# Linear attention and mixer in one kernel: batch 0's residual taken from a turned copy instead of from TensorE, with a new order of the engines' work

## The chip, the cores and the metric

The kernel runs on one core of a Trainium2 chip. The metric is device time in microseconds (us): one launch, as the slowest (here the only) core takes it.

## The reference

Inputs are `r`, `k`, `v` of shape 4 x 8 x 768 x 48 (batch, heads, steps, head size), the decay `w` and the bonus `u` (8 x 48), and four mixer weights. For each batch and head a state of 48 x 48 runs over the steps:

```
y[t]  = r[t] @ (state + (u*k[t]) outer v[t])
state = w * state + k[t] outer v[t]
```

The heads' outputs, side by side, are `x` (4 x 768 x 384). The mixer follows:

```
h   = relu(x^T @ w_tok1) @ w_tok2      # over the 768 steps, hidden 256
u   = x + h^T
out = u + relu(u @ w_ch1) @ w_ch2      # over the 384 channels, hidden 1536
```

The output is float32; TensorE works in bf16.

## The kernel before, in words

A batch's 768 steps are six chunks of 128. A chunk (or, for batch 0, a pair of chunks at once) goes through: products of `k` and `r` with decay tables (`kr`, on POOL or VectorE), a turn of them so that channels lie on partitions (by TensorE into `tr_ps`/`trk` for batches 0 and 1, by a DMA transpose `turn_rk` into `rk` for batches 2 and 3), scores on TensorE (`at_ps`) and their mask on VectorE (`AT`), the state's update (`kv_ps`), and the output `y_ps`, which ends as `x_b`.

The mixer of a batch follows: `hid` (h_ps, six chunks by w_tok1), a ReLU to `h1r`, then per half of the batch (sg = 0, 1, three chunks each) the sum `u`. Where `(b, sg)` is in `DIRECT`, TensorE makes `u` turned: `turn_x` and `back` into `hx_ps`, copied to `uT`. Elsewhere `back` makes `hT_ps`, VectorE adds `x_b` into `u_sb`, and the DMA transpose `turn_u` on SP's queue turns it into `uT`. From `uT` come twelve `up` groups a half (three matmuls of 128 x 384 each, `z_ps`, then a ReLU to `zr`), and three output tiles a half, each of three `down` groups of four matmuls (`h_ps`; the group that begins at j0 uses weight block w4, w5 or w6 for j0 = 0, 4, 8). The output tile still lacks the residual `u`. It comes in one of two ways:

```
by_res = [direct[sg] and (b, sg) not in BACK for sg in range(2)]
# by_res: in down(), after the last group, three matmuls of uT with the identity into the same bank;
#         sum_o() is then a copy, on ScalarE or VectorE as ENGINES says
# else:   sum_o() is a VectorE add of h_ps and u_sb; where the half is DIRECT, u_sb is uT turned back:
def turn_back(sg):
    def f():
        M["u", sg] = sb("u_sb", [128, 3, dm], bf16)
        sp.dma_start_transpose(M["u", sg].rearrange("p c (m d) -> p (c m) d", m=3),
                               M["uT", sg].rearrange("p c m t -> p (c m t)"))
    return f
```

The order of everything is written out. The code adds 880 tasks (a task is a few instructions of one engine), numbered as they are added; `ORDER` (line 22) lists the numbers, and the tasks are emitted in that order and kept in it on every engine, on POOL's queue and on SP's, which issues all loads, stores and transposes. `BUFS` gives the buffer of each allocation, `ENGINES` the engine of each task that may run on two. `WAITS` (line 130) makes some DMAs wait for others: the load of batch 1's first v tile waits for weight block w2, for instance. `FILL` (line 139) adds matmuls on a constant tile `warm` ahead of the tasks it names. The seven weight transfers w0 to w6 (w0, w1 tokens; w2, w3 up; w4 to w6 down) are issued by POOL, in its order with its products.

Numbers that come up later, in the old numbering: 116 and 117 are w5 and w6; 318 is the product of k of batch 1, chunk 1, 63 its load, 62 the load of v of batch 1, chunk 0; 599 is the `back` of batch 2, chunk 4, 603 the `turn_u` of batch 2, second half, 604 and 628 the first `up` of its two halves; 781 is the last `back` of batch 3, 783 the `turn_u` of its second half, 784 and 808 the first `up`s.

Of the kernel before, what the change touches and what calls it, by code (L numbers as in the profile page):

```python
# [62 lines left out]
    0, 1, 2, 3, 4, 5, 0, 1, 2, 3, 5, 4, 0, 1, 3, 2, 5, 4, 0, 1, 3, 5, 4, 2,  # L63
    ],
# [8 lines left out]
    ],  # L73
    'kp': [
    0, 1, 2, 3, 4, 5, 1, 3, 4, 0, 2, 5, 3, 2, 1, 4, 5, 2, 1, 3, 0, 5, 4, 1, 3, 2, 0,
    ],
    'p': [
    0, 1, 2, 3, 4, 5, 0, 2, 0, 3, 1, 4, 2, 0, 5, 3, 1, 4, 2, 0, 5, 3, 4, 1,
    ],
    'a': [  # L80
    0, 1, 2, 3, 4, 5, 6, 7, 8, 9, 10, 2, 0, 1, 4, 3, 6, 7, 5, 10, 2, 8, 9, 3, 1, 0, 4, 6, 7, 2, 5, 8, 10, 9, 3, 2, 7,
    8, 1, 0, 4, 6, 5, 10, 3, 2, 9, 7, 1, 8, 0, 4, 10, 6, 5, 9, 2, 7, 3, 0,
    ],
    'e': [
    0, 1, 2, 3, 4, 5, 6, 7, 8, 9, 10, 11, 0, 1, 2, 3, 4, 5, 10, 9, 0, 2, 6, 8, 7, 3, 4, 10, 2, 6, 8, 7, 9, 10, 2, 3,
    4, 6, 7, 9, 6, 8, 4, 11, 7, 5, 9, 8, 6, 4, 7, 0, 6, 7, 9, 8, 7, 11, 0, 9, 6, 8, 7, 5, 10, 3, 2, 11, 0, 1, 9, 6, 8,
    7,
# [8 lines left out]
    0, 1, 2, 3, 4, 5, 6, 7, 8, 9, 10, 11, 0, 2, 1, 3, 4, 5, 6, 7, 8, 9, 10, 11, 1, 3, 5, 6, 0, 8, 9, 2, 4, 7, 10, 11,  # L96
    ],
    'g': [
    0, 1, 2, 3, 4, 5, 0, 1, 2, 4, 3, 5, 0, 1, 2, 3, 0, 4, 1, 2, 5,
# [5 lines left out]
    0, 1, 2, 3, 4, 5, 6, 1, 0, 2, 3, 4, 5, 6, 1, 2, 0, 4, 3, 5, 6, 2, 1, 4,  # L105
    ],
    'u': [
    0, 1, 2, 3, 4, 5, 6, 7, 1, 0, 2, 5, 4, 3,
# [6 lines left out]
    ],  # L115
}
ENGINES = [
# [18 lines left out]
WIDE_AT = [  # L136
    0, 1, 2, 3, 4, 5, 6, 7, 8, 9, 10, 11, 12,
]
FILL = {132: 3, 140: 3, 206: 1, 879: 1}
POOL_ONLY = [2, 3]  # L140
PAIRED = [(0, 0), (0, 1), (0, 2)]
GB = [2, 2, 3, 3]
# [13 lines left out]
PART = 4  # L156
STORE = ['SP', 'SP', 'SP', 'SP']
WIDE_K = [2, 3]
BACK = [(1, 0)]
MASK_LATER = []  # L160
END = 256
CAST = []
# [1093 lines left out]
```

## Time and profile before

| | |
|---|---|
| runs | 159.94, 159.95, 160.15 us; median 159.95 |
| span of the profiled execution | 158.2 us (its own time is one of those above; about 1.75 us lie around the span) |
| instructions | 4001 |
| busy in the span | TensorE 151.8 us, VectorE 107.0, POOL 90.1, ScalarE 77.7 |
| DMA | 27.39 MB, mean 173 GB/s |
| granted TensorE clock | 0.998 of full speed |

PE is TensorE's matmuls, PEld its weight loads, DVE is VectorE, ACT ScalarE, POOL GpSimd, SP SyncE; a q behind an engine is its queue or sequencer. All instructions stand on line 239, the helper that records the order, so groups and waits are told apart by their tiles (out<-in). A row of the timeline or of the chain begins with its start and its length; in square brackets stands how long the engine was idle before it and what ended that. Rows of groups end with busy time, mean length in ns, idle time before and its cause. A matmul's length holds its way through the array; how far apart they start is seen from row to row.

### The profile page before, as it was taken

To read this page: it belongs to the slowest core of one execution; us is meant where nothing else is said; L and a number is where in the kernel's file an instruction comes from. 1 tells how busy PE (TensorE), PEld (TensorE's weight loads), DVE (VectorE), ACT (ScalarE), POOL (GpSimd) and SP (SyncE) were. 2 spreads that over 40 slices of the span, in tenths; PEclk is the share of its full clock that TensorE was granted. 3 is DMA by queue.
4 is the path that set the end of the run, shared out by engine and by line. 5 is a ranking of instruction groups with operands and counts; after the bars stand their busy time and mean duration, and the time that the engine had idled before them with its cause. 6 is when DMAs were issued, how large, how long until landed. Compare 5 with 4: busy or idle time off the path is not lost.

```text
span 158.2 us, 4001 instructions
## 1 busy us (share of the span) xinstructions
PE 151.8 (96%) x1574; PEld 101.3 (64%) x1574; DVE 107.0 (68%) x218; ACT 77.7 (49%) x187; POOL 90.1 (57%) x120
## 2 busy tenths in 40 slices
PE   6988999999999999999999999999999999999991
PEld 1356767776767676666677665576666566666660
DVE  2689992468967994467989637898987465432071
ACT  3677797737990581478476440235643102463000
POOL 7859969444183799999928999398920000000000
PEclk9999999999999999999999999999999999999999
DMA  4999999999989999999999989999992075300044
GB/s 125 265 261 264 205 204 210 229 204 210 227 176 187 203 230 195 187 210 136 220 194 173 227 158 129 190 193 215 145 274 101 29 176 146 126 0 4 0 151 147
DMA packets 88148, 27.39 MB, mean 173 GB/s; under 512 B 82753, under 2 KB 87234, under 8 KB 88130
## 3 DMA queue, kind: packets, MB, share of 16 engines
q1 hardware_dynamic: 85776, 23.86, 76.1%
q0 software_dynamic: 2160, 3.15, 11.7%
q8 instruction: 12, 0.20, 0.5%
q10 hardware_dynamic: 194, 0.14, 0.3%
q14 instruction: 6, 0.05, 0.1%
HBM read 20.65 MB, written 4.72 MB: 160 GB/s over the span
## 4 chain that ended last, share of the span: by engine, by line
PE 87%; DVE 4%; DMA 3%; POOL 2%; ACT 1%; issue 1%; POOLq 0%; ACTq 0%
PE h_ps L239 35%; PE z_ps L239 29%; PE y_ps L239 6%; PE at_ps L239 4%; PE kv_ps L239 3%; PE hT_ps L239 3%; PE hx_ps L239 3%; DVE kr L239 3%; DMA uT<-u_sb 3%; PE tr_ps L239 2%; PE ad_ps L239 1%; PE trk L239 1%; POOL mask L239 1%; ACT rka L239 1%; POOL bm L239 1%
## 5 line engine op out<-in xcount | busy, mean ns | idle before, releaser
L239 PE MATMUL h_ps<-wch,zr 128*128 128x384 bf16 (+2 forms) x300 | 53.4, 319 | 0.0
L239 PE MATMUL z_ps<-uT,wch 128*128 128x384 bf16 x288 | 52.4, 327 | 0.3 <-DMA uT<-u_sb 0.3
L239 ACT ACTIVATE zr<-z_ps 128x384 bf16<-128x384 f32 x63 | 28.7, 492 | 36.1 <-PE z_ps L239 35.9
L239 PEld LDWEIGHTS <-wch 128*128 128x128 bf16 x288 | 31.1, 114 | 13.4 <-DMA uT<-u_sb 0.7
L239 PEld LDWEIGHTS <-zr 128*128 128x128 bf16 x300 | 27.6, 98 | 15.7
L239 DVE TENSOR_TENSOR AT<-at_ps,mask 128x512 bf16<-128x512 f32 x48 | 30.6, 682 | 2.2 <-PE at_ps L239 2.2
L239 DVE TENSOR_SCALAR zr<-z_ps 128x384 bf16<-128x384 f32 x33 | 17.7, 554 | 13.5 <-PE z_ps L239 13.5
L239 POOL TENSOR_TENSOR yd<-vb,adg 128x384 f32<-128x384 bf16 x13 | 10.6, 829 | 10.8 <-ACT vb L239 5.9
L239 DVE TENSOR_TENSOR osb<-u_sb,h_ps 128x384 f32<-128x384 bf16 (+2 forms) x19 | 10.0, 531 | 9.6 <-PE h_ps L239 9.0
L239 PEld LDWEIGHTS <-kr 128*128 128x128 bf16 (+1 forms) x196 | 11.6, 97 | 3.9 <-DVE kr L239 0.7
L239 POOL TENSOR_TENSOR kr<-rt,wp 128x384 bf16<-128x384 f32 x12 | 12.0, 1005 | 3.1 <-DMA rt<-in_r_dram 3.1
L239 POOL TENSOR_TENSOR ku<-kw,u_bc 128x384 f32<-128x384 f32 x12 | 11.9, 1003 | 2.4 <-DMA u_bc<-in_u_dram 2.4
L239 DVE TENSOR_TENSOR u_sb<-x_b,hT_ps 128x384 bf16<-128x384 bf16 x15 | 7.9, 550 | 6.5 <-PE hT_ps L239 6.4
L239 POOL TENSOR_TENSOR rku<-ku,rt 128x384 f32<-128x384 f32 x12 | 12.0, 1002 | 0.2
L239 POOL TENSOR_TENSOR kr<-kw,wnat 128x384 bf16<-128x384 f32 x12 | 12.0, 1004 | 0.0
L239 ACT CAST vb<-vt 128x384 bf16<-128x384 f32 x18 | 9.0, 513 | 2.5 <-DMA vt<-in_v_dram 2.5
L239 PEld LDWEIGHTS <-wtok 128*128 128x128 bf16 x78 | 7.3, 98 | 4.1
L239 DVE TENSOR_TENSOR x_b<-y_ps,yd 128x384 bf16<-128x384 f32 x18 | 9.4, 551 | 0.6 <-PE y_ps L239 0.5
L239 ACT ACTIVATE yd<-vb,adg 128x48 f32<-128x48 bf16 x40 | 9.5, 322 | 0.1
L239 ACT COPY rkb<-tr_ps 128x1024 bf16<-128x1024 bf16 x6 | 6.1, 1013 | 6.7 <-PE tr_ps L239 6.7
L239 PE MATMUL h_ps<-x_b,wtok 128*128 128x384 bf16 x48 | 8.8, 326 | 0.0
L239 PE MATMUL y_ps<-vb,AT 128*128 128x48 bf16 (+1 forms) x240 | 8.4, 182 | 0.0
(99 smaller groups left out, 190.8 us busy)
## 6 DMA issues: line engine op xcount, KB each, us to landing
out_dram<-osb SPq DMA_DIRECT2D x23, 192.0 KB, 2.6
vt<-in_v_dram SPq DMA_DIRECT2D x18, 192.0 KB, 3.5
win<-in_r_dram SPq DMA_DIRECT2D x6, 384.0 KB, 6.2
kw<-in_k_dram SPq DMA_DIRECT2D x12, 192.0 KB, 4.6
rt<-in_r_dram SPq DMA_DIRECT2D x12, 192.0 KB, 4.0
wch<-in_moe_w_ch_dram POOLq DMA_DIRECT2D x4, 384.0 KB, 6.4
win<-in_k_dram SPq DMA_DIRECT2D x3, 384.0 KB, 5.7
win<-in_v_dram SPq DMA_DIRECT2D x3, 384.0 KB, 7.1
```

The lines of the kernel that those rows point to most:

```text
L239: return lambda *args, **kw: tc.keep_in_program_order(f(*args, **kw))
```

## The change

`BACK` gets both halves of batch 0. So the 18 residual matmuls go, two transposes `turn_back` join SP's queue (the new tasks 219 and 229, which moves all later numbers by 1 and then by 2), and the six evacuations of batch 0 are VectorE adds that also wait for these transposes; four of them were ScalarE copies. `FILL` keeps one entry. The whole `ORDER` is another, with the buffers that go with it, and twelve tasks change engines: the four evacuations (ScalarE to VectorE), `bm` (POOL to VectorE), four products of batch 1 (VectorE to POOL), a copy of batch 1 and two ReLUs of batch 2 (VectorE to ScalarE). Cut to what is spoken of:

```
 ORDER = [
...
-    308, 65, 227, 228, 309, 252, 234, 253, 314, 256, 235, 68, 320, 258, 116, 232, 259, 115, 240, 64, 229, 233, 260,
...
-    73, 315, 264, 316, 239, 275, 317, 262, 265, 251, 341, 343, 266, 117, 342, 326, 267, 329, 327, 50, 270, 67, 351,
...
-    686, 498, 100, 602, 599, 713, 494, 600, 719, 698, 603, 495, 604, 700, 689, 499, 605, 705, 106, 721, 626, 108, 699,
-    610, 694, 290, 716, 618, 706, 703, 622, 619, 724, 628, 623, 608, 629, 714, 616, 725, 500, 614, 609, 646, 617, 745,
...
+    209, 309, 213, 315, 216, 226, 211, 32, 221, 341, 217, 222, 223, 218, 214, 212, 224, 342, 215, 227, 225, 62, 310,
+    228, 73, 230, 311, 63, 254, 236, 255, 316, 37, 234, 50, 237, 65, 272, 48, 235, 262, 231, 320, 343, 273, 263,
...
+    355, 245, 246, 49, 335, 333, 232, 117, 69, 332, 325, 250, 116, 336, 233, 276, 356, 326, 334, 347, 321, 74, 274,
...
+    463, 100, 689, 102, 687, 690, 590, 490, 591, 695, 494, 693, 698, 592, 713, 703, 593, 594, 704, 596, 595, 742,
+    599, 597, 603, 491, 598, 715, 495, 492, 600, 721, 500, 103, 688, 601, 604, 496, 691, 602, 700, 497, 605, 702,
+    501, 696, 630, 106, 708, 606, 716, 701, 626, 108, 607, 631, 628, 718, 292, 624, 502, 104, 717, 625, 726, 612,
...
-FILL = {132: 3, 140: 3, 206: 1, 879: 1}
+FILL = {879: 1}
...
-BACK = [(1, 0)]
+BACK = [(0,0),(0,1),(1,0)]
```

More of the change, by code (lines that the diff above doesn't have):

```diff
@@ L62 @@
     'w': [
-    0, 1, 2, 3, 4, 5, 0, 1, 2, 3, 5, 4, 0, 1, 3, 2, 5, 4, 0, 1, 3, 5, 4, 2,
+    0, 1, 2, 3, 4, 5, 1, 0, 2, 3, 5, 4, 1, 0, 2, 3, 5, 4, 0, 1, 5, 2, 4, 3,
     ],
     'm': [
[7 rows of a table removed]
[7 rows of a table added]
     ],
     'kp': [
-    0, 1, 2, 3, 4, 5, 1, 3, 4, 0, 2, 5, 3, 2, 1, 4, 5, 2, 1, 3, 0, 5, 4, 1, 3, 2, 0,
+    0, 1, 2, 3, 4, 5, 1, 3, 4, 0, 2, 5, 3, 4, 1, 0, 1, 2, 4, 5, 3, 0, 1, 2, 4, 5, 3,
     ],
     'p': [
-    0, 1, 2, 3, 4, 5, 0, 2, 0, 3, 1, 4, 2, 0, 5, 3, 1, 4, 2, 0, 5, 3, 4, 1,
+    0, 1, 2, 3, 4, 5, 1, 3, 2, 1, 0, 2, 4, 3, 5, 1, 0, 2, 4, 3, 1, 5, 2, 0,
     ],
     'a': [
-    0, 1, 2, 3, 4, 5, 6, 7, 8, 9, 10, 2, 0, 1, 4, 3, 6, 7, 5, 10, 2, 8, 9, 3, 1, 0, 4, 6, 7, 2, 5, 8, 10, 9, 3, 2, 7,
-    8, 1, 0, 4, 6, 5, 10, 3, 2, 9, 7, 1, 8, 0, 4, 10, 6, 5, 9, 2, 7, 3, 0,
+    0, 1, 2, 3, 4, 5, 6, 7, 8, 9, 10, 0, 1, 2, 3, 4, 5, 6, 7, 0, 8, 9, 10, 2, 1, 3, 5, 6, 4, 8, 10, 0, 7, 0, 9, 2,
+    4, 8, 1, 3, 5, 6, 10, 2, 7, 0, 9, 1, 4, 3, 8, 5, 6, 2, 10, 0, 9, 1, 7, 3,
     ],
     'e': [
-    0, 1, 2, 3, 4, 5, 6, 7, 8, 9, 10, 11, 0, 1, 2, 3, 4, 5, 10, 9, 0, 2, 6, 8, 7, 3, 4, 10, 2, 6, 8, 7, 9, 10, 2, 3,
-    4, 6, 7, 9, 6, 8, 4, 11, 7, 5, 9, 8, 6, 4, 7, 0, 6, 7, 9, 8, 7, 11, 0, 9, 6, 8, 7, 5, 10, 3, 2, 11, 0, 1, 9, 6, 8,
-    7,
+    0, 1, 2, 3, 4, 5, 6, 7, 8, 9, 10, 11, 0, 1, 2, 3, 4, 5, 9, 8, 10, 0, 11, 6, 5, 1, 0, 5, 3, 0, 9, 11, 6, 1, 3, 0,
+    9, 5, 6, 6, 11, 0, 8, 6, 5, 0, 11, 8, 6, 8, 10, 8, 0, 1, 10, 0, 8, 1, 10, 0, 8, 11, 9, 4, 3, 1, 7, 10, 0, 11, 9,
+    6, 4, 8,
     ],
@@ L95 @@
     'l': [
-    0, 1, 2, 3, 4, 5, 6, 7, 8, 9, 10, 11, 0, 2, 1, 3, 4, 5, 6, 7, 8, 9, 10, 11, 1, 3, 5, 6, 0, 8, 9, 2, 4, 7, 10, 11,
+    0, 1, 2, 3, 4, 5, 6, 7, 8, 9, 10, 11, 0, 3, 2, 1, 5, 6, 4, 7, 8, 9, 10, 11, 3, 0, 2, 1, 6, 5, 4, 7, 8, 9, 10, 11,
     ],
     'g': [
-    0, 1, 2, 3, 4, 5, 0, 1, 2, 4, 3, 5, 0, 1, 2, 3, 0, 4, 1, 2, 5,
+    0, 1, 2, 3, 4, 5, 0, 1, 2, 3, 4, 1, 0, 5, 2, 4, 3, 0, 1, 5, 2,
     ],
@@ L104 @@
     'v': [
-    0, 1, 2, 3, 4, 5, 6, 1, 0, 2, 3, 4, 5, 6, 1, 2, 0, 4, 3, 5, 6, 2, 1, 4,
+    0, 1, 2, 3, 4, 5, 6, 0, 1, 2, 3, 4, 5, 6, 0, 2, 1, 4, 3, 5, 6, 0, 2, 4,
     ],
     'u': [
-    0, 1, 2, 3, 4, 5, 6, 7, 1, 0, 2, 5, 4, 3,
+    0, 1, 2, 3, 4, 5, 6, 7, 0, 1, 3, 2, 4, 7, 6, 5,
     ],
```

97 rows, old and new, of tables (BUFS, ENGINES, ORDER) are left out of this document.

## The prediction

> **What bounds the kernel now.** First the page: the span, the busy shares and the chain that ended last. Then the stretches, to see where TensorE has room.
>
> ```profile
> span 158.2 us, 4001 instructions
> PE 151.8 (96%) x1574; PEld 101.3 (64%) x1574; DVE 107.0 (68%) x218; ACT 77.7 (49%) x187; POOL 90.1 (57%) x120
> PE 87%; DVE 4%; DMA 3%; POOL 2%; ACT 1%; issue 1%; POOLq 0%; ACTq 0%
> 0.00:22.50 22.50, 19.94 (x321) 11.80 (x322) 17.79 (x40) 15.40 (x28) 18.18 (x42) 1.00 1.13 222
> 22.50:45.08 22.58, 22.58 (x252) 16.15 (x252) 15.76 (x33) 17.05 (x41) 11.73 (x14) 1.00 1.09 210
> 45.08:102.47 57.39, 57.09 (x597) 38.59 (x593) 42.12 (x85) 28.16 (x78) 47.42 (x52) 1.00 1.08 189
> 102.47:154.70 52.23, 52.21 (x413) 34.72 (x413) 30.93 (x61) 17.08 (x43) 12.74 (x14) 1.00 0.52 123
> ```
>
> In a row of stretches the first number after the bounds is its length, the next TensorE's busy time; the three last are granted clock, DMA share and GB/s. From 22.5 us to the last matmul TensorE stands still for 0.3 us in 132. So any TensorE work taken out there comes off the time, and any wait put in there is added to it. The DMA share is above 1 up to 102 us: what is issued later than before also lands later. The three runs shown are 159.94 to 160.15 us, median 159.95; the span is 158.2, so 1.75 us lie around it, which I leave as they are. I sum against 159.95.
>
> **What is taken out.** Eighteen 128-column matmuls add the residual of batch 0 (three for each of six output tiles). Seven fill matmuls go too.
>
> ```profile
> 65.24 0.82 PE h_ps L239 x7
> 72.59 0.65 PE h_ps L239 x4
> 10.86 0.81 PE L239 MATMUL at_ps<-warm 128*128 128x512 bf16 x3
> 13.55 0.65 PE L239 MATMUL kv_ps<-warm 128*128 128x384 bf16 x3
> 24.95 0.33 PE L239 MATMUL h_ps<-warm 128*128 128x384 bf16 x1
> 25.12 0.81 PE L239 MATMUL h_ps<-x_b,wtok 128*128 128x384 bf16 x4
> ```
>
> In the chain four down matmuls take 0.65 us, and four with three residual ones 0.82: 0.17 for three, six times, **-1.0 us**. The single fill costs 25.12 - 24.95 = **-0.17**. The other six fills are 0.81 and 0.65 us of TensorE's time, but in a start where it also waits (19.94 of 22.5 us busy); the reordered start (POOL's index patterns ahead of its mask, the decay tables in another order) still needs the same loads and VectorE products. I take **-0.5** for the start, a third of the fills' 1.46 (neither end is nearer by a row), between 0 and -1.5. Sum of the gains: -1.67.
>
> **What is only moved.** Four residual evacuations go from ScalarE copies to VectorE adds (4 x 0.55 = 2.2 us), while four products, a copy and two ReLUs leave VectorE: it is lighter. POOL gets the four products at 1.00 us and loses the mask block `bm`. No TensorE wait hangs on these by itself; cover is POOL's own idle time (4.64 us in the row below). If that cover were gone, the weight DMAs queued on POOL would come later, and that is counted below. The two new turning transfers cost SP an issue each (1.63); the rest of the b=1 and b=2 loads queue behind them, and the six adds wait for them while their h_ps banks stay taken. The cover is whatever slack those loads and banks have, and TensorE's list shows none missing between 45 and 98 us. I take 0 and keep 0 to +1.6, one issue, for the range; less than nothing is excluded, since nothing is loaded sooner by it.
>
> ```profile
> L239 DVE TENSOR_TENSOR osb<-u_sb,h_ps 128x384 f32<-128x384 bf16 x17 | 9.3, 551 | 9.1 <-PE h_ps L239 8.6
> L239 POOL TENSOR_TENSOR kr<-kt,wnat 128x384 bf16<-128x384 f32 x4 | 4.0, 1003 | 0.3 <-POOL kr L239 0.2
> 37.90 0.82 POOL L239 TENSOR_TENSOR yd<-vb,adg 128x384 f32<-128x384 bf16 x1 [4.64 <-ACT adg L239]
> 73.93 1.63 SPq L239 DMA_TRANSPOSE u_sb<-uT  x1
> ```
>
> **The orders: three new waits.** TensorE runs its list in order, so I read the new list (task numbers rise by 1 from 219 and by 2 from 228) for places where less TensorE work stands between a result and its return through another engine and a DMA.
>
> First, batch 2, second half. Before, after its last `back` product come a down group, a score block, `up` of the *first* half, a down group, four more `up`s and a y block, and only then the first `up` of the second half. The new list has ... 496 (down), 700 (scores), 501 (down), 630: task 630 is that `up`, and nothing else is ahead of it.
>
> ```profile
> 97.06 0.49 PE L239 MATMUL hT_ps<-h1r,wtok 128*128 128x384 bf16 x2
> 97.38 0.81 PE L239 MATMUL h_ps<-wch,zr 128*128 128x384 bf16 x4
> 98.13 0.62 PE L239 MATMUL at_ps<-rk 64*128 64x128 bf16 x16
> 98.68 0.68 PE L239 MATMUL z_ps<-uT,wch 128*128 128x384 bf16 x3
> 102.47 3.12 PE L239 MATMUL z_ps<-uT,wch 128*128 128x384 bf16 x18 [0.30 <-DMA uT<-u_sb]
> 94.56 1.37 SPq L239 DMA_TRANSPOSE uT<-u_sb  x1
> 98.17 4.26 DMA uT<-u_sb
> uT<-u_sb SPq DMA_TRANSPOSE x1, 3.9
> ```
>
> From the `back` (97.06) to the `up` (102.47) 5.41 us pass, and even then TensorE waits 0.30: the loop back, add, transfer, up is already the limit here. Of the work ahead there stay 98.68 - 97.06 = 1.62 and one down group of 0.65 (as in the chain): 2.27 us. The transfer took 4.26 us; the last row is the landing of the one issued at 94.56, 3.9. One load fewer is queued ahead of it now, so I take 3.9. The add and the issue come 98.17 - 97.06 = 1.11 after the `back`: 1.11 + 3.9 - 2.27 = **+2.8** (2.0 with 3.2, the quickest landing of such a transfer below, to 3.1). ScalarE and VectorE stand idle behind it; late next is their ReLU, which the following `up`s of both halves cover.
>
> Second, batch 3. The new list goes 663, 674 and 664 in old numbers (down groups), then one `up` of each half less than before: 784, 796, and already 808, the first `up` of the second half.
>
> ```profile
> 127.52 0.49 PE L239 MATMUL hT_ps<-h1r,wtok 128*128 128x384 bf16 x2
> 129.13 1.32 SPq L239 DMA_TRANSPOSE uT<-u_sb  x1
> uT<-u_sb SPq DMA_TRANSPOSE x1, 3.3
> uT<-u_sb SPq DMA_TRANSPOSE x1, 3.2
> 112.17 0.49 PE z_ps L239 x3
> ```
>
> Needed: 129.13 + 3.3 - 127.52 = 4.9 us. There: 0.33 for the `back`, three down groups of 0.65 and two `up`s of 0.49, 3.26. **+1.5** (1.0 if the add is 0.5 us quicker, to 1.7).
>
> Third, the down weights of batch 0. In the new POOL order the second block (`w5`) comes last, after `w6`, behind six products, of which the first (b=1, chunk 1) needs a load that SP now issues after the blocked one.
>
> ```profile
> SPq L239 <- DMA wch<-in_moe_w_ch_dram: 8.3, 1, 8.3
> 13.49 5.51 SPq L239 DMA_DIRECT2D kt<-in_k_dram  x3
> 27.32 0.37 SPq L239 DMA_DIRECT2D vt<-in_v_dram  x1
> win<-in_r_dram SPq DMA_DIRECT2D x1, 384.0 KB, 6.3
> 32.10 1.15 POOL L239 DMA_DIRECT2D wch<-in_moe_w_ch_dram  x2
> wch<-in_moe_w_ch_dram POOLq DMA_DIRECT2D x2, 384.0 KB, 6.0
> wch<-in_moe_w_ch_dram POOLq DMA_DIRECT2D x1, 384.0 KB, 5.8
> wch<-in_moe_w_ch_dram POOLq DMA_DIRECT2D x1, 768.0 KB, 8.3
> 45.08 0.81 PE L239 MATMUL h_ps<-wch,zr 128*128 128x384 bf16 x4
> ```
>
> SP waits 8.3 us for a weight and goes on at 27.32. Before, that k tile was one of the three issued from 13.49; now it is the third transfer behind the wait. The same 576 KB went out there before as a v tile and a `win` issued at 27.79, which landed 6.3 later: 34.1. Then POOL needs five products of 1.00, one of 0.82 and one weight issue of 0.6 before `w6` (0.6) and `w5`: issue of `w5` at 41.1. Blocks of this size landed 5.0 to 7.0 us after issue in the pair (mean 6.0), 5.8 alone: I take 6.5 for the second of a pair, 47.6. TensorE uses it first at 45.08; now a score block (0.55) and a down group (0.65) stand ahead and 0.08 less, and the start gained 0.67: 45.5. **+2.1** (0.5 with 5.0, 3.9 with 8.3; 0 if the k tile lands 2 us sooner).
>
> The rule of the Trainium skill in "DMA: Bandwidth & Descriptors", section "Anatomy of one DMA", speaks here for the change: about 2.0 us fixed plus bytes over 436 GB/s, so an estimated 2.9 us for such a block. By it `w5` lands at 44 and the third wait is gone. The rows say 5.0 and more, with the DMA share above 1, and I go by them.
>
> **Sum.** 159.95 - 1.0 - 0.17 - 0.5 + 2.8 + 1.5 + 2.1 = 164.7 us.
>
> **Rivals.** (A) The weights land in time, the two turned operands do not: without the third wait 162.6. For it: POOL's chain hangs on one load's landing, which I only infer. (B) Other side: the turning transfers land early enough to cost nothing. This needs less than 1.2 us from issue to landing in batch 2; the gains alone then give 158.3. It decides for "faster" when the three waits together stay under 1.67 us. Against it: no such landing is below 3.2. (C) The new gap of about 3 us lets the granted clock fall, and the following `up`s run at half rate. The start shows half rate: the ten 512-column fills there.
>
> ```profile
> 3.80 4.06 PE L239 MATMUL kv_ps<-warm 128*128 128x512 bf16 x10
> ```
>
> Ten in 4.06 us are 0.41 each, where three of the same size at 10.86 take 0.81 with their drain. Half rate for 4.06 us once more loses 2.0: 166.7. Against it: the granted clock reads 1.00 in every stretch up to 154.7. "TensorE: Matmul & The Clock Gate" in the Trainium skill (Part 1) sets the idle window at about 3.4 us, which an estimated gap of 2.8 us would just miss; no row here has a gap that long. (D) The residual transfer fails to hide: loads for batch 2 come 1.5 us later and TensorE waits for scores as well: 164.7 + 1.6 = 166.3.
>
> **How the numbers follow.** The three waits: 0.58, own range 163.2 to 166.2. A 0.20, B 0.09, C and D 0.05 each; 0.03 that waits and gains cancel. The range must leave out no more than 2 in 10: from 161.4 (A with its shortest waits) to 166.7 (C and D). A difference of 0.2% is about what this measurement can tell: faster is B and a part of the cancelling case, 0.10; same 0.04; slower 0.86.
>
> **What would show it.** Right: no `h_ps<-ident,uT` group; two more `u_sb<-uT` transfers; in the waits, TensorE or its weight loads on DMA uT twice, 2 to 3 and 1 to 2 us, at the first second-half `z_ps` of batches 2 and 3; one wait of `h_ps` on DMA wch near 46; TensorE busy down by 1.5 to 2.3. Wrong: TensorE without gaps after 22 us (B), or a gap at another place, above all at scores of batch 2 (D), or a clock below 1.00 (C).

## The result, and the profile after

| | before | after |
|---|---|---|
| median of the runs | 160.05 us (159.94 to 160.36) | 175.56 us (172.61 to 177.27) |
| ratio | | 1.084, 95% interval 1.076 to 1.093 |
| span of the profiled execution | 158.2 us | 174.3 us |
| granted clock | 0.998 | 0.971 (0.989 and 0.978 in two other runs) |

The change makes the kernel slower, as forecast, but by 13.5 us (by the ratio) or 15.5 us (by the medians) instead of 4.7. Medians are of all runs, while ratios leave out runs more than 1.5% above the fastest of their kernel, here those of 176.03 us (the profiled one) and 177.27 us. The runs of after differ by up to 4.7 us, and the granted clock differs with them, which the section on the clock explains in part.

First the page of after: span, busy line, clock line, chain.

```profile
span 174.3 us, 3956 instructions
PE 157.2 (90%) x1548; PEld 102.7 (59%) x1549; DVE 107.6 (62%) x218; ACT 77.0 (44%) x186; POOL 93.0 (53%) x121
PEclk9999999999996999999999999659999999999999
PE 59%; DMA 18%; DVE 12%; issue 4%; POOL 3%; ACT 2%; SPq 0%; POOLq 0%; ACTq 0%; DVEq 0%
```

TensorE does less work than before (1548 instructions, not 1574) and is busy 5.4 us longer: part of it ran at a lower clock, which the clock line shows at two places. In the chain the share of DMA has gone from 3% to 18%. Next what TensorE waited for (us in total, times, longest).

```profile
PE z_ps L240 <- DMA uT<-u_sb: 6.1, 3, 4.2
PE h_ps L240 <- DMA wch<-in_moe_w_ch_dram: 1.8, 1, 1.8
PE kv_ps L240 <- DVE warm L240: 1.3, 1, 1.3
PE wd_ps L240 <- DMA wp<-in_w_dram: 1.0, 1, 1.0
PE ad_ps L240 <- DVE pr L240: 0.8, 1, 0.8
PE z_ps L240 <- DMA wch<-in_moe_w_ch_dram: 0.7, 1, 0.7
```

The three waits that were forecast are there, in the first two rows. Their places, in the timeline of TensorE and in the chain of after (the `h_ps` row at 106.35 is the last work ahead of the long one):

```profile
51.92 1.35 PE L240 MATMUL h_ps<-wch,zr 128*128 128x384 bf16 x4 [1.85 <-DMA wch<-in_moe_w_ch_dram]
106.35 0.82 PE L240 MATMUL h_ps<-wch,zr 128*128 128x384 bf16 x4
111.42 6.76 PE L240 MATMUL z_ps<-uT,wch 128*128 128x384 bf16 x24 [4.25 <-DMA uT<-u_sb]
148.33 3.93 PE L240 MATMUL z_ps<-uT,wch 128*128 128x384 bf16 x23 [1.42 <-DMA uT<-u_sb]
...
44.98 6.90 DMA wch<-in_moe_w_ch_dram
106.13 5.24 DMA uT<-u_sb
145.07 3.21 DMA uT<-u_sb
```

The 24 up matmuls at 111.42 take 6.76 us, 0.28 each; 23 at 148.33 take 3.93, 0.17 each. Behind the long wait TensorE ran at half rate.

To see where 16.1 us came from I cut both profiles at rows that both have: the first up group of batch 0 and the first hidden matmuls of batches 1, 2 and 3. TensorE's timeline, before, then after:

```profile
29.72 2.11 PE L239 MATMUL z_ps<-uT,wch 128*128 128x384 bf16 x12
60.18 2.11 PE L239 MATMUL h_ps<-x_b,wtok 128*128 128x384 bf16 x12
89.24 2.11 PE L239 MATMUL h_ps<-x_b,wtok 128*128 128x384 bf16 x12
121.34 2.11 PE L239 MATMUL h_ps<-x_b,wtok 128*128 128x384 bf16 x12
```

```profile
32.11 2.11 PE L240 MATMUL z_ps<-uT,wch 128*128 128x384 bf16 x12
66.62 2.12 PE L240 MATMUL h_ps<-x_b,wtok 128*128 128x384 bf16 x12
97.73 2.11 PE L240 MATMUL h_ps<-x_b,wtok 128*128 128x384 bf16 x12
136.03 2.11 PE L240 MATMUL h_ps<-x_b,wtok 128*128 128x384 bf16 x12
```

Lengths of the five stretches, worked out from such rows, for these two kernels and for the experiments that follow (each from its one profiled execution; u1's, 173.61 us, is the longest of its four, the others took 168.06 to 169.23):

| kernel | start | to batch 1 | to batch 2 | to batch 3 | to the end | span |
|---|---|---|---|---|---|---|
| before | 29.7 | 30.5 | 29.1 | 32.1 | 36.9 | 158.2 |
| after | 32.1 | 34.5 | 31.1 | 38.3 | 38.3 | 174.3 |
| h1_start | 29.8 | 38.7 | 32.3 | 35.7 | 38.3 | 174.8 |
| h2_first_batch | 29.7 | 31.8 | 30.7 | 36.4 | 38.3 | 166.9 |
| h3_three_batches | 29.7 | 35.1 | 28.7 | 31.7 | 38.6 | 163.9 |
| e1_change_alone | 29.8 | 35.5 | 28.7 | 32.4 | 36.7 | 163.0 |
| u1_one_up | 32.3 | 36.3 | 32.0 | 33.0 | 38.3 | 171.9 |
| g1_up_early_in_before | 29.7 | 30.5 | 29.1 | 37.3 | 36.9 | 163.4 |
| w2_both_first | 32.4 | 31.1 | 32.9 | 36.6 | 38.3 | 171.3 |
| k1_three_moves | 34.8 | 30.9 | 32.5 | 32.9 | 37.5 | 168.6 |
| k2_moves_and_start | 30.4 | 37.6 | 33.6 | 32.4 | 37.5 | 171.6 |

After against before: +2.4, +4.0, +2.0, +6.2, +1.4. The forecast had -0.7 for the start, +1.4 to batch 1 (2.1 less four of the six residual groups), -0.3 to batch 2 (the other two groups), +2.8 to batch 3 and +1.5 to the end.

### The profile page after: what moved, and what is told of

The parts are those of the page before. It is cut to its first block, busy times and chain, and to the rows that moved or that the text cites. A ratio compares the mean times of both kernels' runs of the same rounds, so it can differ in the third digit from the quotient of the medians.

```text
span 174.3 us, 3956 instructions
## 1 busy us (share of the span) xinstructions
PE 157.2 (90%) x1548; PEld 102.7 (59%) x1549; DVE 107.6 (62%) x218; ACT 77.0 (44%) x186; POOL 93.0 (53%) x121
## 4 chain that ended last, share of the span: by engine, by line
PE 59%; DMA 18%; DVE 12%; issue 4%; POOL 3%; ACT 2%; SPq 0%; POOLq 0%; ACTq 0%; DVEq 0%
PE h_ps L240 24%; PE z_ps L240 23%; DMA wch<-in_moe_w_ch_dram 9%; DMA uT<-u_sb 5%; DVE AT L240 4%; PE y_ps L240 3%; PE hT_ps L240 3%; DVE kr L240 2%; PE at_ps L240 2%; DMA wp<-in_w_dram 2%; DMA rk<-kr 2%; PE tr_ps L240 1%; DVE adg L240 1%; DVE u_sb L240 1%; POOL ydb L240 1%
## 5 line engine op out<-in xcount | busy, mean ns | idle before, releaser
L240 PE MATMUL z_ps<-uT,wch 128*128 128x384 bf16 x288 | 54.4, 339 | 7.0 <-DMA uT<-u_sb 6.1
L240 ACT ACTIVATE zr<-z_ps 128x384 bf16<-128x384 f32 x65 | 29.1, 494 | 42.3 <-PE z_ps L240 42.1
L240 PEld LDWEIGHTS <-wch 128*128 128x128 bf16 x288 | 31.6, 116 | 23.2 <-DMA uT<-u_sb 7.3
L240 DVE TENSOR_TENSOR AT<-at_ps,mask 128x512 bf16<-128x512 f32 x48 | 30.5, 682 | 4.8 <-PE at_ps L240 4.7
L240 DVE TENSOR_SCALAR zr<-z_ps 128x384 bf16<-128x384 f32 x31 | 16.4, 555 | 20.7 <-PE z_ps L240 20.7
L240 DVE TENSOR_TENSOR osb<-u_sb,h_ps 128x384 f32<-128x384 bf16 (+2 forms) x25 | 13.2, 534 | 12.8 <-PE h_ps L240 12.4
L240 PEld LDWEIGHTS <-kr 128*128 128x128 bf16 (+1 forms) x196 | 13.3, 105 | 4.1 <-issue 1.1
L240 POOL TENSOR_TENSOR kr<-win,wpair 128x384 bf16<-128x384 f32 x8 | 8.1, 1043 | 0.8 <-DMA win<-in_r_dram 0.8
```

Source lines behind the costliest of these rows:

```text
L240: return lambda *args, **kw: tc.keep_in_program_order(f(*args, **kw))
```

## The clock: half rate by fixed stretches of 3.41 us

The records of the granted clock change only at multiples of 3.413 us within a profile. After goes to full rate at 11.09 us (before at 7.34), falls to half at 52.05 for one such stretch and at 110.07 for two. The windows of after, cut at these bounds (length, TensorE busy, ..., clock, DMA share, GB/s):

```profile
48.64:52.05 3.41, 1.56 (x27) 1.13 (x22) 2.95 (x5) 2.52 (x9) 1.45 (x2) 1.00 1.12 217
52.05:55.46 3.41, 3.41 (x23) 2.51 (x22) 0.44 (x2) 0.87 (x1) 0.00 (x0) 0.50 1.09 199
...
106.66:110.07 3.41, 0.52 (x4) 0.10 (x1) 2.17 (x4) 0.00 (x0) 2.31 (x3) 1.00 1.22 85
110.07:113.48 3.41, 2.06 (x7) 1.03 (x8) 0.87 (x2) 0.00 (x0) 0.58 (x1) 0.50 1.19 212
113.48:116.90 3.42, 3.42 (x13) 1.52 (x11) 1.77 (x4) 0.94 (x3) 2.64 (x3) 0.50 1.35 231
116.90:120.31 3.41, 3.41 (x26) 2.41 (x25) 0.00 (x0) 1.32 (x4) 1.05 (x2) 1.00 0.89 201
...
144.21:147.62 3.41, 2.71 (x17) 1.50 (x15) 2.32 (x5) 0.49 (x1) 0.00 (x0) 1.00 0.73 186
```

In these traces what a stretch does sets the rate of the next. Busy 1.56 or 0.52 of 3.41: half rate follows. The gap of 1.42 us in batch 3 lies across a bound (147.62), leaves 2.71 busy, and nothing follows. Half the busy time of a half-rate stretch is lost, 1.7 us if it is full: here (3.41 + 2.06 + 3.42) / 2 = 4.4 us. The bounds lie elsewhere in each trace, so the same gap costs 0, 1 or 2 stretches (the wait for w5: none in r1 and f1, one in after, two in u1); (1 - clock) x 2 x span / 3.41 gives 3.0 stretches for the runs of 176.03 and 177.27 us, 2.2 for 175.10 and 1.1 for 172.61. So about two stretches, 3.2 us, of the spread of 4.7 us are the clock's; the rest I have not placed. The windows of three experiments below bear it out from both sides:

```profile
47.62:51.03 3.41, 1.78 (x36) 1.33 (x33) 2.90 (x5) 2.87 (x11) 1.80 (x3) 1.00 1.11 218
51.03:54.44 3.41, 3.35 (x34) 2.44 (x34) 1.60 (x5) 1.84 (x3) 0.75 (x1) 1.00 1.03 178
```

```profile
48.29:51.70 3.41, 1.64 (x32) 1.19 (x27) 2.95 (x5) 2.73 (x10) 1.64 (x2) 1.00 1.07 200
51.70:55.11 3.41, 2.78 (x28) 2.06 (x28) 1.04 (x3) 1.27 (x2) 0.18 (x1) 1.00 0.99 196
```

```profile
48.46:51.87 3.41, 1.16 (x20) 0.88 (x19) 2.83 (x5) 2.25 (x8) 1.16 (x2) 1.00 1.26 161
51.87:55.28 3.41, 2.59 (x17) 1.90 (x17) 0.00 (x0) 0.00 (x0) 0.00 (x0) 0.50 1.23 214
```

They are r1 (busy 1.78, full rate follows), f1 (1.64, full) and u1 (1.16, half), all at the same wait for w5. Busy time gives no sharp limit, though. In q1, another experiment below, 1.65 us were followed by half rate:

```profile
56.56:59.97 3.41, 1.65 (x29) 1.09 (x29) 1.63 (x5) 1.83 (x3) 2.03 (x3) 1.00 1.19 225
59.97:63.38 3.41, 3.41 (x38) 2.43 (x36) 3.23 (x8) 2.49 (x10) 3.41 (x4) 0.50 1.36 214
```

From the first up group on, in the traces of all twenty kernels, every full-rate stretch with 1.56 us busy or less was followed by half rate and every one with 1.73 or more by full rate; f1 (1.64) and q1 (1.65) lie between and went different ways. "TensorE: Matmul & The Clock Gate" in the Trainium skill (Part 1) has the window, 3413 ns and free-running, and the traces agree; its rule that the clock falls after an idle window of about 3.4 us does not fit, since 1.85 us of idle time were enough at 52.05.

## Experiments

Task numbers are those of the changed kernel unless said otherwise. Times are medians; intervals are 95%, of the ratio to before; a comparison of two experiments goes by their ratios.

**Order or change, stretch by stretch.** Three kernels start in the order of before and go on in that of after; a fourth has the order of before throughout, with the change put in. The fills are those of before (one of a warm task stands at the task that after gives it).

```diff
 e1: ORDER, ENGINES of before; BACK of after; SP: 67, +219, 69, 78, 74, 47, 84, 75, 72, 76, +229, 82
 h1: like e1 up to task 230 (first up of batch 0), then the order of after
 h2: like e1 up to task 426 (first up of batch 1), then the order of after
 h3: like e1 up to task 769 (hidden matmuls of batch 3), then the order of after
```

> Order, engines and fills of before up to the first up group of batch 0 (29.72 us in before, 32.11 in after), the order of after from there on. Theory: only the start is mended, the first up group comes 2.4 us earlier, and the three waits and both stretches of half rate behind it stay: 175.6 - 2.4 = 173.2 us, 171 to 175. Rival (the start's loss is made up later anyway, because the weights and transfers that TensorE waits for do not come sooner): 175 to 176.

> Order, engines and fills of before up to the first up group of batch 1, the order of after from there on. Theory: besides the start, the waits on the weights (0.73 and 1.85 us) and the stretch of half rate behind the second (clock 0.50 to 0.55 from 52.0 to 55.5 us, 1.7 us lost) go: 173.2 - 4.3 = 168.9 us, 167.5 to 170.5; the wait of batch 2 (4.25 us) and half rate behind it stay. Rival (turning transfers cost by themselves): 171 or more, with waits on DMA before 66 us.

> Order, engines and fills of before up to the hidden matmuls of batch 3, the order of after from there on. Theory: the wait of batch 2 (4.25 us against 0.30) and half rate behind it (clock 0.50 from 110.1 to 116.7 us, 24 up matmuls in 6.76 us instead of 3.9) go as well; left is the wait of batch 3 (1.42 us): 159.1 + 1.4 = 160.5 us, 160.0 to 161.3. Rival (the clock falls for another reason than the gaps): 163 or more with a clock below 0.99.

> The order, engines and fills of before, with nothing but the change of the residual: BACK for both halves of batch 0, the two turning transfers put into SP's order behind the loads 67 and 76 (about 38 and 45 us), and the six evacuations VectorE adds. Theory (the loss is the new order's: three late places, the start, and the clock after the gaps): 18 residual matmuls of 0.055 us go and nothing waits, 160.05 - 1.0 = 159.1 us, 158.9 to 159.6. Rival (the turning transfers themselves cost: in the trace of after SP spends 5.73 and 2.88 us on issuing them, and the loads of batches 1 and 2 queue behind): 161.5 or more, with new waits of TensorE between 45 and 98 us.

Measured: h1 175.57 us, ratio 1.094 (1.088 to 1.100); h2 168.93, 1.050 (1.044 to 1.057); h3 164.57, 1.014 (1.005 to 1.022); e1 162.73, 1.010 (1.005 to 1.015). h2 came as expected. h1 did not, and its rival held: the start is mended (29.8 us) and all of it is lost in the next stretch (38.7 instead of 34.5), where TensorE waits 2.17 us for a `kr` of POOL and 1.90 for w5, and two of the clock's stretches are at half rate instead of one. So up to batch 1 the loads and POOL set the pace in the order of after. And e1, where I expected a gain, is slower than before by about 1%. Its DVE timeline and TensorE's:

```profile
58.83 0.55 DVE L241 TENSOR_TENSOR osb<-u_sb,h_ps 128x384 f32<-128x384 bf16 x1 [2.65 <-DMA u_sb<-uT]
59.44 0.33 PE L241 MATMUL y_ps<-S,rkb 128*128 128x96 bf16 x4 [3.26 <-DVE osb L241]
```

The second turning transfer goes out at 54.97 and lands at 58.81; VectorE's add waits for it, the mask products behind it wait too, and TensorE with them. h3 has the same wait, 3.7 us, and so missed the 160.0 to 161.3 us of its theory.

**The misplaced up group.** u1 mends it in after, g1 puts it into before (old numbers there).

```diff
-u1, PE: 630, 606, 626, 628, 624, 612, 614, 644
+        606, 626, 628, 624, 612, 614, 630, 644
-g1, PE: 494, 698, 604, 499, 626, 610, 618, 703, 622, 628, 608
+        494, 698, 499, 628, 604, 626, 610, 618, 703, 622, 608
```

> The changed kernel with a single TensorE task moved (and its ReLU on VectorE with it): the first up of batch 2's second half goes behind six ups of the first half instead of ahead of them. Theory: the first half's transfer went out at 103.05 us and has landed by 107 to 108.3, so TensorE goes on within 1.1 us of 107.17; six ups of 0.49 then cover the second half's landing at 111.4 but for 0.2 to 1.3 us. Of the wait of 4.25 us 1.4 stays, in two pieces, and the clock does not fall (2.7 us): 175.6 - 2.85 - 2.7 = 170.0 us, 168.5 to 172.5. Rival (what is late is the DMA queues as a whole, the first half's transfer too): a wait of 3 us or more stays and with it half rate, 174 to 176.

> The kernel before with one TensorE task moved to where the changed kernel has it (and its ReLU with it): the first up of batch 2's second half comes directly after the last two down groups, ahead of the first up of the first half and of all the rest. Theory (the prediction's first step, by itself): its wait grows by 2.8 us, 160.3 + 2.8 = 163.1 us where the idle time falls into two of the clock's stretches of 3.41 us, and 1.7 us more for each stretch of half rate: 163 to 166.5. Rival (in the order of before the transfer lands sooner, or VectorE and the loads gain by the pause): 160 to 162.

Measured: u1 169.20 us, 1.053 (1.049 to 1.058); g1 165.67, 1.034 (1.031 to 1.037). Both came as the theory said. In g1 the wait and the half rate behind it stand by themselves (timeline, then windows):

```profile
102.70 0.91 PE L241 MATMUL z_ps<-uT,wch 128*128 128x384 bf16 x3 [3.16 <-DMA uT<-u_sb]
104.26 3.15 PE L241 MATMUL z_ps<-uT,wch 128*128 128x384 bf16 x12 [0.65 <-DVE zr L241]
```

```profile
99.59:103.00 3.41, 0.30 (x2) 0.26 (x3) 0.00 (x0) 0.00 (x0) 1.39 (x2) 1.00 1.38 182
103.00:106.41 3.41, 2.76 (x10) 1.18 (x9) 2.76 (x5) 0.49 (x1) 2.84 (x4) 0.50 1.03 191
```

3.16 - 0.30 = 2.9 us of wait, 2.76 / 2 = 1.4 by the clock, 0.65 for a ReLU that now comes late: 4.9, and the stretch to batch 3 grew by 5.2. One of TensorE's tasks, moved with its ReLU, costs this.

**Is it the gap that lowers the clock?** Fill matmuls in the gap of batch 2, ahead of the score block of two chunks there; each count is issued for both chunks.

```diff
-FILL = {879: 1}
+FILL = {879: 1, 700: 18}     # f1: 36 fills
+FILL = {879: 1, 700: 9}      # f2: 18 fills
```

> The changed kernel with 18 fill matmuls of 512 columns (about 0.22 us each at full rate, 3.9 us in all) put ahead of the score block that comes before the gap of batch 2; nothing else. The end of the wait cannot come sooner by it (it hangs on the transfer at 106.13 us, which the fills do not hold up). Theory (the clock falls because TensorE stood idle): the granted clock stays 1.00 there, the 24 up matmuls behind it take 3.9 us instead of 6.76, 175.6 - 2.7 = 172.9 us, 171.5 to 174. Rival (the clock falls at this place for another reason): clock 0.50 for some 6 us all the same, 175 to 177.

> As the run with fills in the gap of batch 2, with 9 in place of 18 on each of the score block's two chunks (there the fills came twice, 8.1 us for a gap of 4.25; the 24 up matmuls behind took 4.06 us, but began 2.3 us later). Now 18 fills of 0.22 us, 3.9 us. Theory: the fills end before the transfer lands (111.4 us), the clock stays 1.00, the 24 matmuls take 4.06 instead of 6.76 us: 175.6 - 2.7 = 172.9 us, 171 to 174.5. Rival (the fills hold up the mask products and with them something behind): 175 or more.

Measured: f1 176.25 us, 1.096 (1.090 to 1.103); f2 172.30, 1.064 (1.060 to 1.068), against 1.084 for after. f1 had twice the fills that I meant, 8.1 us of them, and so began the ups 2.3 us later; but its 24 up matmuls took 4.06 us. f2 keeps the clock there:

```profile
106.86:110.27 3.41, 3.41 (x24) 1.37 (x24) 1.15 (x2) 0.00 (x0) 0.71 (x1) 1.00 1.26 77
111.80 4.09 PE L241 MATMUL z_ps<-uT,wch 128*128 128x384 bf16 x24 [0.43 <-DMA uT<-u_sb]
```

The wait still ends when the transfer lands, so the fills hold nothing up that the trace shows. f2's two runs with almost no half rate (clock 0.998 and 0.997) took 170.85 and 170.39 us; after's run of 172.61 us had 1.1 stretches, and without them, 1.9 us, it would be at an estimated 170.7. By the ratios and by the medians work without use in the gap is worth 2% of the kernel. The gap is the cause of the half rate.

**The weights of batch 0.**

```diff
-after, POOL: 320, w4, 387, 353, 319, 379, 345, w6, w5
+w1,    POOL: 320, w4, w5, 387, 353, 319, 379, 345, w6
+w2,    POOL: 320, w4, w5, w6, 387, 353, 319, 379, 345
```

> The changed kernel with one POOL task moved: the DMA of weight block w5 is issued right behind w4 (38.4 us) instead of behind six products and w6 (44.98 us). Theory: w5 lands 6 to 7 us after about 39.0, at 45 to 46, before TensorE's need at 50.07: the wait of 1.85 us goes and with it half rate from 52.0 to 55.5 us (1.7 us): 175.6 - 3.5 = 172.1 us, 170.5 to 173.5. Rival (the wait moves on to w6, which then lands last, near 52, and is needed within a group or two): 174 to 176.

> The changed kernel with both w5 and w6 issued by POOL right behind w4, at 39.0 and 39.6 us, instead of at 44.98 and 44.38. With w5 alone in front, w6 landed at 54.35, 9.87 us after its issue, and TensorE waited 2.66 us for it. Theory (what counts is the issue: POOL's products in front of the two blocks): w5 and w6 land by 47 to 49, the wait goes and half rate with it: 175.6 - 3.5 = 172.1 us, 170.5 to 174. Rival (what counts is the traffic: the turning transfer that SP issues from 40.2 us lands beside them, and three blocks at once take longer): the last of them lands at 50 or later, a wait of 1 us or more stays, 174 to 177.

Measured: w1 175.89 us, 1.088 (1.084 to 1.091); w2 173.44, 1.082 (1.078 to 1.085). In w1 the rival held: w6, issued at the same time as in after, took 9.87 us to land instead of 5.52, and TensorE waited 2.66 us for it. In w2 both were issued by 39.5 us and landed at 47.57 and 49.55, the wait is gone and the stretch to batch 1 is 3.4 us shorter; but the next is 1.8 longer (scores and a turned operand of batch 2 late by 1.17 each), and by the ratios w2 and after can't be told apart (after 1.076 to 1.093). What is gained at one place of this part is given back at the next.

**What the change costs by itself.** In the order of before: the second transfer earlier (e2), the first half alone (b1), and both or the first on ScalarE's queue (q1, q2), where ScalarE stood idle. And after without it (r1).

```diff
 e2: like e1, SP: 67, 219, 69, 78, +229, 74, 47, 84, 75, 72, 76, -229, 82
 b1: like before; BACK = [(0, 0), (1, 0)]; SP: 67, +219, 69
-                sp.dma_start_transpose(M["u", sg]...
+                (act if b == 0 else sp).dma_start_transpose(M["u", sg]...      # q1: both halves, q2: the first
 r1: like after; BACK = [(1, 0)], ORDER without 219 and 229
```

> As the run with the change alone (order of before), but the turning transfer of the second half of batch 0 goes out eight transfers earlier in SP's order, at about 48 us instead of 54.97. There its landing at 58.81 held VectorE's add for 2.65 us, with a mask product and TensorE's y_ps (3.26 us) queued behind it. Theory (the change itself is worth its 1.0 us where its transfers are early enough for VectorE's order): no wait on u_sb, 160.2 - 1.0 = 159.2 us, 158.8 to 159.8. Rival (any place on SP's queue costs, because the issue takes 1.9 to 3.8 us there and the loads of batch 2 come that much later): TensorE waits for scores of batch 2, or VectorE for another load, 160.5 to 162.5.

> The order of before with half of the change: BACK for the first half of batch 0 only (one turning transfer, issued near 42 us, nine residual matmuls fewer, three evacuations by VectorE). Theory: this transfer lands before VectorE's first add (48.6 us in the run with the change alone, without a wait), and SP has only 3.8 us to make up: 160.2 - 0.5 = 159.7 us, 159.3 to 160.2. Rival (3.8 us of SP are not free in the order of before either: a v tile or a k tile of batches 1 and 2 comes late, as in the run with the earlier transfer): 160.6 to 162.

> The change alone in the order of before, with the two turning transfers of batch 0 issued by ScalarE's queue instead of SP's, where ScalarE stands idle in before (near 34 us, and near 47.2 us behind a v copy; idle there 1.95 and 4.36 us). Theory (what the change costs is its place in SP's queue: 1.9 to 3.9 us of issue each, with the loads of batches 1 and 2 behind): the loads keep their times, nothing waits, 160.3 - 1.0 = 159.3 us, 158.9 to 160.0. Rival (what costs is the transfers' traffic beside the loads, whatever the queue): a v tile or turned operand comes late all the same, 160.8 to 163.

> As the other run of this call, for the first half of batch 0 alone (one transfer, by ScalarE's queue near 34 us, nine residual matmuls fewer). Theory (SP's queue): 160.3 - 0.5 = 159.8 us, 159.4 to 160.3; with the same transfer on SP's queue it was 161.8. Rival (traffic, or ScalarE's ReLUs late behind the issue): 160.6 to 162.

> Order, engines, buffers and fill of the changed kernel, but the residual of batch 0 comes from TensorE again (18 matmuls) and the two turning transfers are left out of SP's order; the six evacuations stay VectorE's, as copies. Theory 1 (the new order alone is late; the transfers cost nothing in it): 175.6 + 1.0 = 176.6 us, 175.5 to 178, w5 lands near 52 as before. Theory 2 (the transfers delay what moves beside them: SP spends 5.73 and 2.88 us on them, and w5 and w6, issued at 44.4 to 45.0 us, land beside the first): w5 lands 1 to 2 us sooner and the loads of batches 1 to 3 come some us earlier; the wait at 51.9 and half rate behind it go, 175.6 + 1.0 - 3.5 = 173.1 us, 171 to 174.5.

Measured: e2 163.31 us, 1.019 (1.014 to 1.024); b1 161.81, 1.004 (1.001 to 1.008); q1 165.54, 1.033 (1.028 to 1.038); q2 164.17, 1.024 (1.019 to 1.029); r1 174.27, 1.089 (1.084 to 1.093). In the order of before the change lost time in all five forms; e2, q1 and q2 came out above even the ranges of their rivals. In e2 no add waits 2.65 us any more; a v tile came late instead, and another at 79.53:

```profile
47.67 3.60 SPq L241 DMA_TRANSPOSE u_sb<-uT  x1
59.22 0.33 PE L241 MATMUL kv_ps<-vb,kr 128*128 128x96 bf16 x4 [2.26 <-ACT vb L241]
```

Off SP's queue it got worse, so the queue's order is not all of the cost. In q2, ScalarE's, POOL's and TensorE's timelines:

```profile
34.67 1.44 ACTq L241 DMA_TRANSPOSE u_sb<-uT  x1
43.80 0.98 POOL L241 TENSOR_TENSOR kr<-kt,wnat 128x384 bf16<-128x384 f32 x1 [4.47 <-DMA kt<-in_k_dram]
44.84 0.55 PE L241 MATMUL trk<-ident,kr 128*128 128x128 bf16 x4 [2.28 <-POOL kr L241]
```

That one transfer took 9.91 us to land, the last down block issued 4 us later 9.11 (5.82 in before), and a k tile held up POOL for 4.47. While it was under way, from 34.67 to 44.58 us, the DMA engines moved 160 GB/s at a share of 1.16; in the same stretch of before they moved 213 at 1.09. The rival "traffic" held: the transfer lies among loads that fill the DMA engines, and they come later. r1 has the new order without the change, and is 8.9% slower than before; e1 has the change without the new order, and is 1.0% slower. So nearly all of the loss is the new order's. r1's time lies in the range of its second theory, but its wait for w5 stayed (1.68 us). Whether the change gains or costs time in the order of after these runs can't tell (r1 against after). I know no order in which its 1.0 us is gained.

**The fills.**

```diff
-FILL = {132: 3, 140: 3, 206: 1, 879: 1}     # before
+FILL = {879: 1}                             # v1
```

> The kernel before with the seven fill matmuls left out that the change drops (three each ahead of two start tasks, one at the hidden matmuls of chunk 4). Theory (the prediction's gains of 0.17 and 0.5 us): 160.2 - 0.67 = 159.5 us, 158.7 to 160.1. Rival (the six start fills keep the clock up: without them a window with too little work falls into the first 15 us, and half rate costs 1.7 us): 160.6 to 162.5.

Measured: 160.88 us, 1.0036 (1.0009 to 1.0063). Not faster; three of the twelve runs took 162.4 to 162.8 us with a clock of 0.976 to 0.979, two stretches of half rate. This is what the rival said, for a part of the runs; where in them the stretches fell is not known, since the profiled run has none. In that run the first up group came 0.09 us earlier than in before (29.63, not 29.72).

**Do the places add up?**

```diff
 k1: after with u1 and w2, and PE: 806, 804, 788, 808, 802, 800, 792, 794, 796, 790, +810, 814   (810 stood first)
 k2: k1 with order, engines and fills of before up to task 230
```

> The changed kernel with three moves together: the first up of the second half behind six ups of the first in batch 2, the same in batch 3 (behind ten), and w5 and w6 issued right behind w4. Theory (these are separate late places): -6.4 (alone measured, 175.6 to 169.2), -2.1 (alone, 175.6 to 173.4) and -1.4 (the wait before the second half's first up in batch 3): 165.7 us, 163.5 to 167.5. Rival (the places hide each other, and another transfer is late next, scores or ReLUs of batch 2): 168 or more.

> The run with the three moves, and in addition order, engines and fills of before up to the first up group of batch 0. Theory (the start's 2.4 us are a loss of their own, which showed nothing when it was mended alone because the weights came last then): 165.7 - 2.4 = 163.3 us, 162 to 164.5. Rival (it is made up again: POOL's products for batch 1 and SP's loads set the pace up to the first groups of batch 1, whatever the start): 165 or more, with TensorE waiting for kr or v of batch 1.

Measured: k1 169.22 us, 1.057 (1.053 to 1.061), no better than u1 alone (1.053); k2 172.86, 1.076 (1.072 to 1.081). Both rivals held. In k1 the waits for w5 and in batch 3 are gone, but ReLUs are late by 0.65 at two places, scores by 0.99 and a mask product by 0.92, and in the profiled run one stretch of the start fell to half rate (34.8 us to the first up group). In k2 POOL's products wait for loads again, and w5 and w6, issued at 38.9 and 39.5 us, landed at 54.48 and 56.51:

```profile
36.36 0.61 PE L241 MATMUL tr_ps<-ident,kr 128*128 128x128 bf16 x4 [2.14 <-POOL kr L241]
54.52 0.81 PE L241 MATMUL h_ps<-wch,zr 128*128 128x384 bf16 x4 [2.27 <-DMA wch<-in_moe_w_ch_dram]
```

No version beat the kernel before.

## Why the prediction was right or wrong

- **First wait, +2.8.** Right in place and cause: g1 measured 2.9 in the order of before. The working was off by a little: 1.11 + 3.9 - 2.27 is 2.74, and 0.30 of it was there before, so 2.4 were added by it; g1's transfer took 4.45 us where I took 3.9 from a row of before. In after the wait grew by 4.25 - 0.30, because the transfer took 5.24 us. The ReLU behind it, which I held to be covered, came 0.65 us late in g1.
- **Second wait, +1.5.** Right: 1.42, with a landing of 3.2 us (I took 3.3). My own terms, 4.9 - 3.26, give 1.6.
- **Third wait, +2.1.** Right in size (1.85) and by its mechanism: POOL stood 2.89 us for a k tile, and w5 was issued last, at 44.98 and not 41.1; TensorE came later too (50.07, not 45.5), which I had not put in. That the size came out is partly luck: both ends were some 4 us late. The wait of 0.73 for the second up block was not foreseen.
- **The clock: the step that failed most.** Rival C stood at 0.05 with one stretch of 2.0 us; I let a gap of 2.8 us pass because it was shorter than the window of 3.4. Three stretches fell to half rate in the profiled run, 4.4 us, two of them at the place that C named, one behind the third wait. f2 shows the cause, g1 the price in a kernel without other faults.
- **The start, -0.5, and the fill, -0.17.** Wrong in sign. v1 shows no gain from fewer fills, and the new start costs 2.4 us. In it ScalarE's `lnwd` chain and TensorE's `wd_ps` come early and wait 0.96 us for a load, and full rate comes at 11.09 instead of 7.34 us. Which of the two costs more was not tried.
- **"I take 0" for the turning transfers and moves.** Wrong in the order of before: e1 lost 1% where the gains alone would have given 0.6% (about 2.6 us apart, beyond my bound of 1.6). The cover that I named, the slack of loads and banks, was not there: the DMA share of 1.08 to 1.09 between 22.5 and 102 us, which I had quoted, said so. VectorE, which I had called lighter, was busy 107.6 us instead of 107.0. In the order of after the cost can't be told from the gain (r1).
- **The sum.** Terms were added as if each were its own. Up to batch 2 they were not: in h1, w1, w2, k1 and k2 a place is mended and most of the gain is lost at the next transfer.

The forecast added 4.7 us, the profiled run has 16.1. Of the 11.4 us between them the clock is 4.4, the start 3.1 (2.4 in place of -0.7), the first wait 1.2 and the waits on weights 0.5.

Of the 16.1 us of the profiled run the trace places: start 2.4, waits on weights 2.6, waits in batches 2 and 3 5.4, half rate 4.4, less the residual's 1.0: 13.8. Some 2 us, most of it between the hidden matmuls of batches 1 and 2, I have not placed; 0.5 of it is a wait for a turned operand at 84.54, and work that the new order moved from one stretch to another is in it.

## What to carry to other kernels

Count, for each result that returns by a DMA, the TensorE work between its product and its first use: one group too early costs the missing microseconds. Then lay the clock's stretch over the gap: here about 1.8 us of idle time within one stretch of 3.41 was enough to halve the rate of the next, and matmuls without use, put where they hold nothing up, avoided that. Where the DMA share was above 1, a transfer that saves TensorE time was paid for by the loads beside it, whichever queue issued it. And mending one late place shows little where the loads set the pace (h1, w1, w2), but some 5 us, by the ratios, where one group was misplaced (u1).

## What the hardware showed that I had not expected

- Behind the first up group the granted clock fell after each fixed stretch of 3.41 us in which TensorE was busy 1.56 us or less, after none with 1.73 or more, and after one of two between (1.65 in q1, not 1.64 in f1). From half rate it did not come back after a stretch with 2.59 us busy (u1) or 2.06 (after), and did after 2.76 (g1). In the start, with its small matmuls, it fell once even after 1.95 busy (k1), so busy time alone is not the measure.
- The runs of after spread by 4.7 us, of which about 3 follow from how many stretches fell to half rate (1.1 to 3.0). The four runs of before beside them, without such gaps, lay within 0.42 us.
- SP needed between 1.5 and 9.4 us to issue one turning transfer (9.4 in w2, with three weight blocks issued beside it); the same kind of transfer landed 3.2 us after issue in batch 3 and 9.9 us after it in q2. A weight block of 384 KB took 5.0 (before) to 17.1 us (k2).
